# One wo load, the small MLP's end and the stage signals of a staged loop, in a gated attention and token-mixer decode kernel

## The chip, the cores and the metric

The kernel runs on one core of one Trainium2 chip. The metric is the time of one execution on the device in microseconds, the median of several runs. A core has five engines that matter here: PE (matrix products), DVE (vector work), ACT (activations and copies), POOL, and SP, which in this kernel issues nearly all of the transfers between the chip's main memory and the core. The transfers themselves are carried by 16 DMA engines.

## The reference

```python
x = A_x                                              # (1, 1, 448)
g = _sigmoid((x * gate_w).sum(-1, keepdims=True))
# A: 16 query heads, 8 KV heads, 65536 cached positions, head size 256
q = (x @ wq).reshape(B, Sq, Hq, Dh).transpose(0, 2, 1, 3)
k = jnp.repeat(k_cache, 2, axis=1); v = jnp.repeat(v_cache, 2, axis=1)
scores = jnp.einsum("bhqd,bhkd->bhqk", q, k) * (Dh ** -0.5)
o = jnp.einsum("bhqk,bhkd->bhqd", _softmax(scores), v)
a = o.transpose(0, 2, 1, 3).reshape(B, Sq, Hq * Dh) @ wo
# B: a token-mixing MLP on the same token
h = _layernorm(x)
u = _gelu(jnp.einsum("bsd,sf->bdf", h, w1) + b1)     # F = 1792
b = (jnp.einsum("bdf,fs->bds", u, w2) + b2).transpose(0, 2, 1)
return g * a + (1 - g) * b                           # (1, 1, 448), bfloat16
```

The two caches hold 268 MB each and are read once.

## The kernel before, in words

**Blocks.** The 8 KV heads times 65536 positions are cut into 32 blocks of 16384 positions, four to a head. A block has 8.39 MB of K, loaded by load_k in two halves into the two tiles kn0 and kn1 (L123), and 8.39 MB of V, loaded by load_v into the single tile vt (L129). All of them are issued by SP, in program order, on one queue. A tile is loaded again as soon as its last reader is done.

**A block's work.** score_block runs eight steps. A step transposes a slice of K on DVE (transposes, L384; steps 0 to 3 read kn0, steps 4 to 7 read kn1) and then forms eight products on PE (scores, L392). The transposed slices alternate between two buffers, so DVE's step i + 2 waits for PE's step i. softmax takes the maximum of the scores, rescales the running sums and writes the transposed weights pT (L449 to L488). products multiplies pT with V on PE (pv, L412) and adds up on DVE (accumulate, L493). A call may hand score_block a dictionary of hooks: functions whose instructions are put behind step i.

**The loop.** Blocks 0 to 29 run in a loop of 15 iterations with two blocks each (L560). An iteration has four stages: the scores of the first block and the load of its V; then the loads of the next block's K, its softmax and products; and the same two again for the second block. In every second such stage the loop also loads wo of one head (load_wo, L137) into the half wo_sb[:, 1], and in the last stage head_end works on finished heads and lets ACT copy wo_sb[:, 1] to wo_sb[:, 0] (L533), so that after iteration t the half 0 holds wo of head t.

**Stage signals.** The loop is of the staggered kind: an engine enters a stage only when all engines have signalled that they are finished with the stage two before it. By default an engine gives that signal when it comes to the next stage boundary, after it has waited for its own instructions (and on SP its own transfers) of that earlier stage. tc.previous_stage_wait(engine) puts the wait and the signal of one engine at another place in the stage. Waits at the boundary have line L560 in the profile.

**The tail.** Blocks 30 and 31 are written out. Block 30's scores have two hooks: mixer_tail behind step 1 (six DVE instructions, L334 to L345, that end the small MLP and form the gate) and gate_column behind step 2 (a product on PE, L543, that spreads the gate over the partitions, and its copy gcol on DVE, L546). SP issues 3 MB of block 30's V, the two halves of block 31's K, the other 5 MB of that V, and then block 31's V in eight pieces of 2 MB to 256 KB into the K tiles (load_v_last, L146), each when the transposes have freed its place. Behind them come two loads of wo, for heads 14 and 15. The end multiplies the last pieces (columns, L437), forms oT (L633), multiplies it with wo (L639: four products for head 14, four for head 15), copies the row (L645, L646) and stores it (L647).

An order written out by hand (seq) keeps each engine's instructions in program order.

Of the kernel before, what the change touches and what calls it, by code (L numbers as in the profile page):

```python
# [14 lines left out]
HQ = 16  # L15
HKV = 8
DH = 256
REP = HQ // HKV
# [5 lines left out]
NI = VP // NJ  # L24
# [7 lines left out]
def kernel(  # L32
# [28 lines left out]
    def seq(ins):  # L61
        e = ins.ins.engine
        if e in last:
            tc.add_manual_dep(
                ins.ins,
                last[e],
                mybir.DependencyInfo(
                    mybir.DependencyClass.NoSync, mybir.DependencyReason.DATA
                ),
                reason="program order",  # L70
            )
        last[e] = ins.ins.name
        return ins
# [62 lines left out]
    def load_wo(h, r):  # L136
        seq(nc.sync.dma_start(  # L137
            out=wo_sb[:, r],
            in_=A_wo.rearrange("(h p c) n -> h p c n", p=128, c=2)[bass.ds(h, 1)].rearrange(
                "o p c n -> (o p) c n"  # L140
            ),
        ))
# [162 lines left out]
    def place_q(pair):  # L305
        for a in range(NQ):
            quad = slice(32 * a, 32 * (a + 1))
            seq(nc.vector.tensor_copy(  # L308
                out=qz[quad, :, 2 * NI + 32 * a:2 * NI + 32 * a + REP],
                in_=qq_twice[quad, :, bass.ds(pair * REP, REP)],  # L310
            ))
# [21 lines left out]
    def mixer_tail():  # L333
        seq(nc.vector.tensor_scalar(  # L334
            out=gate[:], in0=ez[:], scalar1=1.0, scalar2=None, op0=ALU.add
        ))
        seq(nc.vector.reciprocal(out=gate[:], in_=gate[:]))
        seq(nc.vector.tensor_copy(out=b2f[:], in_=b2b[:]))
        seq(nc.vector.tensor_scalar(  # L339
            out=y_sb[:], in0=y_ps, scalar1=b2f[0:1, 0:1], scalar2=None, op0=ALU.add  # L340
        ))
        seq(nc.vector.tensor_scalar(
            out=rest[:], in0=y_sb[:], scalar1=gate[0:1, 0:1], scalar2=None, op0=ALU.mult
        ))
        seq(nc.vector.tensor_tensor(out=rest[:], in0=y_sb[:], in1=rest[:], op=ALU.subtract))  # L345
# [37 lines left out]
    def transposes(i):  # L383
        seq(nc.vector.transpose(  # L384
            out=kT_tiles[i % 2][:].rearrange("p j w k c -> p (j w k c)").bitcast(FP32),
            in_=k_tiles[i // 4][:, i % 4 * NJ:(i % 4 + 1) * NJ, :].rearrange("p j d -> p (j d)").bitcast(FP32),
        ))

    def scores(e, i):
        for w in range(NW):  # L390
            for c in range(2):
                seq(nc.tensor.matmul(  # L392
                    sc_tiles[e][:, :],
                    lhsT=qz[:, 2 * w + c, 2 * (NI - i):2 * (NI - i) + 128],
                    rhs=kT_tiles[i % 2][:, :, w, :, c],
                    start=(i == 0 and w == 0 and c == 0),
                    stop=(i == NI - 1 and w == NW - 1 and c == 1),
                ))

    def score_block(e, hooks={}):  # L400
        for i in range(NI):
            transposes(i)
            scores(e, i)
            if i in hooks:
                hooks[i]()
# [38 lines left out]
    def softmax(e, fill=None, may_begin=False, pair=None):  # L444
        fill = fill or [lambda: None] * 3
        sc_ps = sc_tiles[e]
        nb, nb_old = nb_tiles[e], nb_tiles[1 - e]
        al, pT = al_tiles[e], pT_tiles[e]
        seq(nc.vector.tensor_reduce(out=rmax[:], in_=sc_ps[:, :], op=ALU.max, axis=AXIS.X))  # L449
        if pair is not None:  # L450
            place_q(pair)
        fill[0]()
        seq(nc.tensor.transpose(sm_ps[0:1, 0:128], rmax[:, 0:1], ident_f[:, :]))  # L453
        fill[1]()
        seq(nc.vector.tensor_reduce(
            out=mnew[:],
            in_=sm_ps[0:1, 0:128].rearrange("o (a i r) -> o r a i", a=4, r=REP)[:, :, :, 0:NI],
            op=ALU.max, axis=AXIS.XY,
        ))
        if may_begin:  # L460
            seq(nc.vector.scalar_tensor_tensor(
                out=mrun[:], in0=mrun[:], scalar=caps[0:1, 1:2], in1=mnew[:],
                op0=ALU.min, op1=ALU.max,
            ))
        else:
            seq(nc.vector.tensor_tensor(out=mrun[:], in0=mrun[:], in1=mnew[:], op=ALU.max))  # L466
        seq(nc.tensor.matmul(  # L467
            sm_ps[:, 128:128 + REP], lhsT=ones_f[0:1, :], rhs=mrun[0:1, :], start=True, stop=True
        ))
        fill[2]()  # L470
        if may_begin:
            seq(nc.vector.tensor_tensor(
                out=nbo[:], in0=nb_old[:], in1=caps[:, 0:1], op=ALU.max
            ))
            nb_old = nbo
        seq(nc.vector.tensor_tensor_reduce(  # L476
            out=junk[:], in0=sm_ps[:, 128:128 + REP], in1=nval[:], scale=1.0, scalar=0.0,
            op0=ALU.mult, op1=ALU.add, accum_out=nb[:, 0:1],
        ))
        seq(nc.scalar.activation(  # L480
            out=p_sb[:, :], in_=sc_ps[:, :], func=ACT.Exp, scale=scale,
            bias=nb[:, 0:1], accum_out=den[:, 0:1],
        ))
        seq(nc.scalar.activation(
            out=al[:], in_=nb_old[:], func=ACT.Exp, scale=-1.0, bias=nb[:, 0:1]
        ))
        seq(nc.vector.transpose(out=pT[:, :], in_=p_sb[:, :]))  # L487
        seq(nc.vector.scalar_tensor_tensor(  # L488
            out=lsum[:], in0=lsum[:], scalar=al[:, 0:1], in1=den[:], op0=ALU.mult, op1=ALU.add
        ))  # L490
# [51 lines left out]
    def gate_column():  # L542
        seq(nc.tensor.matmul(  # L543
            sm_ps[:, 200:201], lhsT=ones_f[0:1, :], rhs=gate[0:1, 0:1], start=True, stop=True
        ))
        seq(nc.vector.tensor_copy(out=gcol[:], in_=sm_ps[:, 200:201]))  # L546
# [10 lines left out]
    mixer_sum()  # L557

    last.clear()
    with tc.For_i(0, HQ - 1, 1, iteration_sync="staggered") as t:  # L560
        for e in range(2):
            if e:
                tc.stage_boundary()
            score_block(e)
            load_v(2 * t + e)
            tc.stage_boundary()
            load_k(2 * t + e + 1, 0)
            load_k(2 * t + e + 1, 1)
            if e == 0:
                load_wo(t, 1)  # L570
                softmax(e, may_begin=True)
                products(e)
            else:
                softmax(e, pair=t + 1)
                denominators()
                products(e)
                head_end()
                turn()
    last.clear()

    for n in (L - 1, L):
        if n < L:
            score_block(n % 2, {1: mixer_tail, 2: gate_column})
        else:
            score_block(n % 2, {1: result_base, 2: lambda: pv(L - 1, 0), 3: lambda: pv_one(L - 1, 2)})
        if n == L - 1:
            load_v(n, 0, 48)
            load_k(L, 0)
            load_k(L, 1)
            load_v(n, 48, VP)  # L590
        else:
            load_v_last(L)
            for h in range(HQ - REP, HQ):
                load_wo(h, h - (HQ - REP))
        if n < L:
            softmax(n % 2)
        else:
            def rest_base():
                for k in range(2):
                    seq(nc.tensor.matmul(  # L600
                        f_rows[k], lhsT=ident_f[0:1, 0:1], rhs=base[0:1, k * MC:(k + 1) * MC],
                        start=True, stop=False, tile_position=(0, 32 * k),
                    ))
                pv(L - 1, 2, range(4, NJ))

            softmax(n % 2, [lambda: pv_one(L - 1, 3), lambda: pv(L - 1, 2, range(4)), rest_base])
            seq(nc.vector.tensor_scalar(
                out=lsv[:], in0=val[:], scalar1=lsum[:, 0:1], scalar2=None, op0=ALU.mult
            ))
            pv(L - 1, 3)  # L610
            accumulate((L - 1) % 2)
            seq(nc.tensor.matmul(
                sm_ps[:, 456:456 + REP], lhsT=ones_f[:, :], rhs=lsv[:, :], start=True, stop=True
            ))
            seq(nc.vector.reciprocal(out=rdv[:], in_=sm_ps[:, 456:456 + REP]))
            seq(nc.vector.tensor_scalar(
                out=rdv[:], in0=rdv[:], scalar1=gcol[:, 0:1], scalar2=None, op0=ALU.mult
            ))
# [59 lines left out]
```

## Time and profile before

| | |
|---|---|
| median of 3 runs | 1268.74 us (1267.89 to 1269.64) |
| the profiled execution | 1268.93 us |
| its span, first to last instruction | 1267.1 us |
| PE busy | 806.4 us (64%) |
| DVE busy | 707.7 us (56%) |
| ACT busy | 58.6 us (5%) |
| read from main memory | 544.45 MB, 430 GB/s over the span |
| mean granted TensorE clock | 0.807 |

The span runs from the first instruction to the last; the execution's own time has some 1.8 us around it. In the profile a line such as "vt<-in_A_v_cache_dram" names a tile and what is written into it. In the chain of waits, each piece is what the next one waited for; "issue" is time in which the engine waited for nothing that the profile shows. In a timeline a row has its start, its length, the engine and line, the tiles, and the number of instructions that are merged in it; the brackets give the idle time before it and what ended it. In a table of windows the columns are the stretch and its length, the busy time of PE, PE's weight loads, DVE, ACT and POOL (with counts), the granted clock, the DMA share and GB/s. The DMA share of a short window can be over 1, since a packet is counted whole where it starts.

### The profile page before, as it was taken

The numbers are of one execution on the slowest core, as the hardware profiler recorded it, in microseconds if no ns is written. First come the engines' busy times: TensorE is split into PE (matmuls) and PEld (weight loads), VectorE is DVE, ScalarE is ACT, GpSimd is POOL, SyncE is SP. The second block draws the span as 40 slices with busy tenths as digits, with TensorE's granted clock in tenths as the row PEclk, the third lists the DMA queues.
The fourth block names the chain that finished last, engine by engine and source line by source line (L and its number), as shares of the span: only waits on it lengthen the run. The fifth ranks groups of instructions, "written<-read, shape, count | busy, mean of one in ns | idle before, by whom it ended". The sixth has DMA issues, their size and how long they took to land.

```text
span 1267.1 us, 12204 instructions
## 1 busy us (share of the span) xinstructions
PE 806.4 (64%) x4689; PEld 321.2 (25%) x4689; DVE 707.7 (56%) x754; ACT 58.6 (5%) x131; POOL 1.7 (0%) x7
## 2 busy tenths in 40 slices
PE   3767665766656566566675675755657665676676
PEld 1222222222222222222222222222222222222223
DVE  4566545565445665456654556644566544665483
ACT  4000000000000000000000000000000000000000
POOL 0000000000000000000000000000000000000000
PEclk9888778788778787787877788777888778787687
DMA  9999999999999999999999999999999999999998
GB/s 413 414 437 444 429 439 418 435 432 446 434 418 437 431 450 432 432 420 432 449 432 435 418 433 434 445 435 418 438 430 447 435 430 424 430 446 435 418 419 343
DMA packets 18306, 544.59 MB, mean 430 GB/s; under 512 B 2421, under 2 KB 4600, under 8 KB 5112
## 3 DMA queue, kind: packets, MB, share of 16 engines
q1 hardware_dynamic: 17858, 544.45, 99.6%
q8 instruction: 6, 0.10, 0.0%
q10 hardware_dynamic: 438, 0.01, 0.0%
q14 instruction: 4, 0.03, 0.0%
HBM read 544.45 MB, written 0.00 MB: 430 GB/s over the span
## 4 chain that ended last, share of the span: by engine, by line
DMA 75%; issue 18%; PE 2%; DVE 2%; SPq 1%; ACT 0%; DVEq 0%
DMA vt<-in_A_v_cache_dram 73%; DMA kn<-in_A_v_cache_dram 2%; DVE kT L384 1%; PE sc L392 1%; PE pv_ps L412 1%; SPq L560 0%; SPq L129 0%; PE hd_ps L528 0%; PE f L639 0%; ACT p_sb L480 0%; DVE acc L493 0%; SPq L146 0%; DVE rmax L449 0%; DVE y_sb L339 0%; PE hd_ps L514 0%
## 5 line engine op out<-in xcount | busy, mean ns | idle before, releaser
L392 PE MATMUL sc<-kT,qz 128*128 128x512 bf16 x2048 | 550.9, 419 | 217.3 <-DVE kT L384 217.1
L384 DVE STREAM_TRANSPOSE kT<-kn 128x2048 f32<-128x2048 f32 x256 | 571.2, 2283 | 109.4 <-DMA kn<-in_A_k_cache_dram 52.6
L392 PEld LDWEIGHTS <-qz 128*128 128x128 bf16 x2048 | 212.7, 104 | 556.1 <-issue 379.4
L412 PE MATMUL pv_ps<-vt,pT 128*4 128x512 bf16 x1968 | 172.5, 526 | 129.0 <-DMA vt<-in_A_v_cache_dram 127.2
L493 DVE SCALAR_TENSOR_TENSOR acc<-acc,al,pv_ps 128x512 f32<-128x512 f32 x31 | 23.2, 748 | 266.5 <-PE pv_ps L412 266.5
L412 PEld LDWEIGHTS <-pT 128*4 128x4 bf16 x2000 | 58.7, 108 | 235.1 <-issue 190.0
L480 ACT ACTIVATE p_sb<-sc,nb 128x512 bf16<-128x512 f32 x32 | 22.0, 687 | 975.6 <-DVE nb L476 975.6
L449 DVE TENSOR_REDUCE rmax<-sc 128x1 f32<-128x512 f32 x32 | 22.1, 692 | 63.6 <-PE sc L392 63.6
L487 DVE STREAM_TRANSPOSE pT<-p_sb 128x512 bf16<-128x512 bf16 x32 | 22.8, 711 | 27.1 <-ACT p_sb L480 27.1
L499 PE MATMUL hd_ps<-lsum,same 128*128 128x1 f32 x30 | 7.4, 315 | 28.8 <-DVE lsum L488 28.8
L467 PE MATMUL sm_ps<-mrun,ones_f 1*128 1x2 f32 x64 | 12.1, 256 | 21.2 <-DVE mrun L466 12.9
L453 PE MATMUL sm_ps<-ident_f,rmax 128*1 128x128 f32 x32 | 8.6, 270 | 24.5 <-DVE rmax L449 24.5
L533 ACT COPY wo_sb<-wo_sb 128x896 bf16<-128x896 bf16 x15 | 14.1, 937 | 199.1 <-PE hd_ps L528 199.1
L514 PE MATMUL hd_ps<-esc,acc 128*128 128x2 f32 x60 | 9.5, 263 | 14.1 <-DVE acc L493 14.1
L528 PE MATMUL hd_ps<-wo_sb,oT 128*1 128x448 bf16 x60 | 17.9, 393 | 0.0
L532 DVE TENSOR_TENSOR a_acc<-a_acc,hd_ps 1x448 f32<-1x448 f32 x15 | 9.1, 608 | 14.5 <-PE hd_ps L528 14.5
L467 PEld LDWEIGHTS sm_ps<-mrun,ones_f 1*128 1x128 f32 x64 | 9.4, 182 | 27.4 <-DVE mrun L466 16.3
L499 PEld LDWEIGHTS hd_ps<-lsum,same 128*128 128x128 f32 x30 | 6.1, 253 | 30.1 <-DVE lsum L488 30.1
L514 PEld LDWEIGHTS hd_ps<-esc,acc 128*128 128x128 f32 x60 | 8.2, 196 | 21.6 <-DVE acc L493 21.6
L476 DVE CUSTOM_DVE_ANT_0 junk<-sm_ps,nval 128x2 f32<-128x2 f32 x32 | 5.1, 160 | 14.0 <-PE sm_ps L467 14.0
L453 PEld LDWEIGHTS sm_ps<-ident_f,rmax 128*1 128x1 f32 x32 | 2.5, 79 | 40.2 <-DVE rmax L449 40.2
L308 DVE COPY qz<-qq 32x16 bf16 (+1 forms) x64 | 10.5, 164 | 1.4
(114 smaller groups left out, 149.5 us busy)
## 6 DMA issues: line engine op xcount, KB each, us to landing
kn<-in_A_k_cache_dram SPq DMA_DIRECT2D x63, 4096.0 KB, 27.3
vt<-in_A_v_cache_dram SPq DMA_DIRECT2D x1, 5120.0 KB
kn<-in_A_k_cache_dram SPq DMA_DIRECT2D x2, 2048.0 KB, 11.9
kn<-in_A_v_cache_dram SPq DMA_DIRECT2D x2, 2048.0 KB, 20.9
wo_sb<-in_A_wo_dram SPq DMA_DIRECT2D x17, 224.0 KB, 27.3
vt<-in_A_wq_dram SPq DMA_DIRECT2D x1, 3072.0 KB, 10.3
vt<-in_A_v_cache_dram SPq DMA_DIRECT2D x1, 3072.0 KB
kn<-in_A_v_cache_dram SPq DMA_DIRECT2D x3, 1024.0 KB, 20.4
```

What stands on the lines that cost most here:

```text
L384: seq(nc.vector.transpose(out=kT_tiles[i % 2][:].rearrange("p j w k c -> p (j w k c)").bitcast(FP32), in_=k_tiles[i // 4][:, i % 4 * NJ:(i ...
L392: seq(nc.tensor.matmul(sc_tiles[e][:, :], lhsT=qz[:, 2 * w + c, 2 * (NI - i):2 * (NI - i) + 128], rhs=kT_tiles[i % 2][:, :, w, :, c], star ...
L412: seq(nc.tensor.matmul(dst[32 * grp:32 * grp + 2 * REP, :, :], lhsT=pT[:, 32 * jj + 2 * REP * ip:32 * jj + 2 * REP * (ip + 1)], rhs=pairs( ...
L449: seq(nc.vector.tensor_reduce(out=rmax[:], in_=sc_ps[:, :], op=ALU.max, axis=AXIS.X))
L467: seq(nc.tensor.matmul(sm_ps[:, 128:128 + REP], lhsT=ones_f[0:1, :], rhs=mrun[0:1, :], start=True, stop=True))
L480: seq(nc.scalar.activation(out=p_sb[:, :], in_=sc_ps[:, :], func=ACT.Exp, scale=scale, bias=nb[:, 0:1], accum_out=den[:, 0:1],))
L487: seq(nc.vector.transpose(out=pT[:, :], in_=p_sb[:, :]))
L493: seq(nc.vector.scalar_tensor_tensor(out=acc[:], in0=acc[:], scalar=al_tiles[e][:, 0:1], in1=src[:, :, :], op0=ALU.mult, op1=ALU.add,))
L499: seq(nc.tensor.matmul(hd_ps[:, 460:461], lhsT=same[:].rearrange("p a r -> p (a r)"), rhs=lsum[:, 0:1], start=True, stop=True,))
L514: seq(nc.tensor.matmul(o_ps[c], lhsT=acc[:, e, :].rearrange("p (d c) -> p c d", c=2)[:, c, :], rhs=weights[:, e, :], start=(start and e == ...
L528: seq(nc.tensor.matmul(a_ps, lhsT=oT[:, c, r:r + 1], rhs=wo_sb[:, r, c, :], start=(r == 0 and c == 0), stop=(r == REP - 1 and c == 1),))
L533: seq(nc.scalar.copy(out=wo_sb[:, 0], in_=wo_sb[:, 1]))
```

## The change

In the two score stages of each iteration, ACT's signal for the stage before is given at the head of the stage, and PE's and DVE's behind step 4 of the eight. In the tail, mixer_tail and gate_column are no longer hooks of block 30's scores but follow its softmax. wo of head 14, which iteration 14 leaves in wo_sb[:, 0], is not loaded a second time.

```diff
     last.clear()
+    def early_signals(i):
+        def both():
+            tc.previous_stage_wait(mybir.EngineType.PE)
+            tc.previous_stage_wait(mybir.EngineType.DVE)
+        return {i: both}
+
     with tc.For_i(0, HQ - 1, 1, iteration_sync="staggered") as t:
         for e in range(2):
             if e:
                 tc.stage_boundary()
-            score_block(e)
+            tc.previous_stage_wait(mybir.EngineType.Activation)
+            score_block(e, early_signals(NI // 2))
             load_v(2 * t + e)
             tc.stage_boundary()
             load_k(2 * t + e + 1, 0)
@@
     for n in (L - 1, L):
         if n < L:
-            score_block(n % 2, {1: mixer_tail, 2: gate_column})
+            score_block(n % 2)
         else:
             score_block(n % 2, {1: result_base, 2: lambda: pv(L - 1, 0), 3: lambda: pv_one(L - 1, 2)})
@@
             load_v_last(L)
-            for h in range(HQ - REP, HQ):
-                load_wo(h, h - (HQ - REP))
+            load_wo(HQ - 1, 1)
         if n < L:
             softmax(n % 2)
+            mixer_tail()
+            gate_column()
         else:
```

## The prediction

> **What bounds the kernel now.** I read the page first (slices and queues), then the chain that ended last, then SP's timeline, then short windows in the tail, and last the trace's DMA packet records (start, length and size of each packet). The page:
>
> ```profile
> DMA  9999999999999999999999999999999999999998
> ...
> DMA packets 18306, 544.59 MB, mean 430 GB/s; under 512 B 2421, under 2 KB 4600, under 8 KB 5112
> ...
> q1 hardware_dynamic: 17858, 544.45, 99.6%
> q8 instruction: 6, 0.10, 0.0%
> ```
>
> Packets fill 99.6% of 16 DMA engines' span. PE is busy 64% and DVE 56%, so neither bounds. The chain of waits shows it again: V transfers of 29 to 34 us and short issues between them.
>
> ```profile
> 603.77 33.72 DMA vt<-in_A_v_cache_dram
> 637.70 8.74 issue
> ...
> 681.99 33.44 DMA vt<-in_A_v_cache_dram
> ```
>
> V lands at 603.77 + 33.72 = 637.49 and, two blocks on, at 681.99 + 33.44 = 715.43. In those 77.94 us the queue moved four 8.389 MB tensors and one 0.229 MB wo load, 33.78 MB: 433.5 GB/s, and other pairs of blocks differ by 0.05 us. Is the queue ever empty? SP's timeline in the loop:
>
> ```profile
> 647.02 0.33 SPq L129 DMA_DIRECT2D vt<-in_A_v_cache_dram  x1
> 667.83 0.94 SPq L123 DMA_DIRECT2D kn<-in_A_k_cache_dram  x2
> 668.97 0.33 SPq L137 DMA_DIRECT2D wo_sb<-in_A_wo_dram  x1
> 681.99 0.33 SPq L129 DMA_DIRECT2D vt<-in_A_v_cache_dram  x1
> ```
>
> The V issued at 647.02 lands at 676.17 (647.02 + the chain's 29.15). K is issued 8.3 us before that, and the next V 13.5 us before that K ends (676.17 + 8.389 MB / 433.5 GB/s = 695.5). In the other half of the iteration K comes 9.9 us (627.63 against 637.49) and V 9.8 us ahead. The loop, 1170 of 1267 us, is one unbroken stream with 8 us to spare.
>
> The tail is not quite that. After block 29's V (landed 1183.07) there come 33.55 MB of K and V, 77.4 us at 433.5, so 1260.5; the last products on V start at 1262.80. Those 2.3 us are all that scheduling can win there. One part shows in half-microsecond windows (the last two columns are DMA share and GB/s):
>
> ```profile
> 1207.00:1207.50 0.50, 0.31 (x2) 0.19 (x2) 0.50 (x2) 0.00 (x0) 0.00 (x0) 1.00 0.46 197
> 1207.50:1208.00 0.50, 0.50 (x4) 0.20 (x3) 0.50 (x1) 0.00 (x0) 0.00 (x0) 1.00 0.24 98
> 1208.00:1208.50 0.50, 0.50 (x4) 0.20 (x3) 0.50 (x1) 0.00 (x0) 0.00 (x0) 1.00 2.34 672
> ```
>
> Most engines run dry for a microsecond, until the K load of block 31 arrives. SP had issued it at 1207.16, right after block 30's fourth transpose freed its tile:
>
> ```profile
> 1193.64 4.50 DVE L384 STREAM_TRANSPOSE kT<-kn 128x2048 f32<-128x2048 f32 x2 [0.16 <-PEq L560]
> ...
> 1199.62 0.61 DVE L345 TENSOR_TENSOR rest<-y_sb,rest 1x448 f32<-1x448 f32 x1
> 1200.17 2.29 DVE L384 STREAM_TRANSPOSE kT<-kn 128x2048 f32<-128x2048 f32 x1
> 1204.76 0.16 DVE L546 COPY gcol<-sm_ps 128x1 f32<-128x1 f32 x1 [2.30 <-PE sm_ps L543]
> 1204.83 4.50 DVE L384 STREAM_TRANSPOSE kT<-kn 128x2048 f32<-128x2048 f32 x2
> ```
>
> **The MLP's end.** It leaves a score block in which it delays DVE. In the loop the third and fourth transposes start 6.03 and 8.94 us after the first (653.33 and 656.24 against 647.30). Here they start 6.53 and 11.19 after it: mixer_tail's six DVE instructions (1198.07 to 1200.23) cost 0.50, and gcol, which waits 2.30 us for a PE product queued behind scores(2), makes it 2.25. Without both, K of block 31 is issued at 1207.16 - 2.25 = 1204.9. Its first packets came 1.0 us after issue (1208.13 in the packet records), so they can start at 1205.9; the first engine runs dry at 1207.24: cover 1.3 us.
>
> What is that worth at the end? By the packet records the engines finished the 3 MB load before it between 1207.24 and 1209.66 (median 1207.65). The next 2 x 2 MB, 9.69 us without a gap, were done at 1218.42 on the first engine and 1218.60 on the median: lost 1.49 and 1.26 us. The two latest engines (1209.29 and 1209.66) lost nothing. Only the engine that ends last counts. It fetched 16 KB of program code at 1245.23 (0.93 us, one of q8's six packets), which put it 1.4 us back, 1.0 behind the next (1247.25 against 1246.23); before that it ran with the pack that had lost 1.2. With the gap closed it is 1.2 us earlier, and an engine that lost nothing, 1.25 us ahead of it, is next. So the term lies between +0.2 (the fetch falls on one of the late engines) and -1.25. I take -0.9, near the row of the engine that did end last, with some allowance for another fetch pattern.
>
> Where the block goes, DVE gets it back: softmax starts 2.25 earlier, then 2.16 us of mixer_tail and some 0.6 for the gate product (0.38), gcol (0.16) and their signals; block 31's first transpose moves from 1221.55 to about 1222.1. Queued behind are block 31's scores on PE and SP's eight V pieces, issued from 1226.08 to 1242.86. The first piece is not needed before block 30's V ends at 1240.4, the last not before 1259: cover 14 us, cost nothing. If that cover were gone it would cost 0.5.
>
> **wo of head 14.** The load goes away, 128 packets of 74 ns, 8 on each engine: 0.59 us of queue time, but behind the last V piece, so V gains nothing. SP saves one 0.33 us issue while it idles. What does gain:
>
> ```profile
> 1263.42 1.04 PE L639 MATMUL f<-wo_sb,oT 128*1 128x224 bf16 x8 [0.25 <-DVE oT L633]
> ...
> 1263.93 0.09 PEld L639 LDWEIGHTS <-oT 128*1 128x1 bf16 x3 [0.24 <-issue]
> ```
>
> The products start in pairs 0.14 us apart (1263.42, 1263.56), so the fifth could start at 1263.70. It starts at 1263.93, just after the second load landed on the slowest engine (1263.89 by its semaphore). One load ends 0.57 earlier and that stall is gone: -0.23. What is late next is oT itself.
>
> **Mid-stage signals.** ACT's signal moves to the head of the score stage, PE's and DVE's behind the fifth of eight steps. SP enters the next stage earlier, so the first K load of a block (its tile is free after four transposes) goes out some 4 to 5 us earlier; the second still waits for the eighth transpose. wo and the next V stay behind them in the same order. The stream was never dry there: 0. Bounds: at the first K of the loop (issued 47.60, wanted from 49.82) the window 49.8 to 50.6 shows a share of 0.87, a possible -0.1 to -0.26 on early engines. Upward, PE and DVE now wait at step five for their own previous stage, over some 14 us before; behind DVE's wait stand three transposes and PE's last scores. Even the 0.5 us that one hook cost would sit under 8.3 us of cover. Should that be gone, it would cost 30 x 0.5 = 15.
>
> By the Trainium skill, "DMA: Bandwidth & Descriptors", Specifications, the fabric into SBUF ends at 435 GB/s; the loop's 433.5 agrees. By it alone (an estimate) no earlier issue in the loop could win more than 0.3% of 1170 us, some 4 us; my sum has none.
>
> **Sum.** -0.9 - 0.23 + 0 = -1.1. The profiled execution took 1268.93 (span 1267.1 and 1.8 around it), 0.2 above the median of 1268.74. So 1267.8 for its like, 1267.6 from the median; I say 1267.7.
>
> **Rivals.**
> *The gap closes for the wrong engines* (0.33): a code fetch meets an engine that was already late, or new addresses move a fetch to the end. For it: three of 16 engines are late, and one fetch (1259.23) lies 3 us before the end. Then only wo's 0.2 remains, or less: 1268.5, between 1268.0 and 1269.4.
> *A queued load has a fixed cost of its own* (0.05): if the removed one cost the 1.0 us from issue to first packet besides its 0.59, and the forecast's 0.9 came on top, 1268.74 - 2.5 = 1266.2. Against it: the last two 256 KB pieces let their products start at 1262.18 and 1262.80, 0.62 apart, and bytes alone make 0.61. The Trainium skill, same page, "Anatomy of one DMA — SWDGE (gpsimd) path", fits 2.0 us plus the bytes to a load issued by GpSimd; by it, as an estimate, this load would be 2.5 us. The row speaks against that for SP's queued loads.
> *The loop's code no longer stays on the chip* (0.04), slower: no 16 KB fetch lies between 50.7 and 1198.6, and the tail, about one iteration's code, made four of 16 KB and three of 8 KB. If moved or added signal instructions push the loop past what is kept, each iteration fetches as much: 4 x 1.4 + 3 x 0.35 = 6.7 us on one or another engine, 15 iterations 100 us, over 16 engines 6.3: about 1275. It decides once any fetch repeats in the loop. Against it: signals move, they do not multiply.
> *The early signals give nothing because SP waits for its own transfers*: also possible, and the time is the forecast's.
>
> **How the numbers follow.** Forecast 0.55 (1266.8 to 1268.3), the first rival 0.33, fixed cost 0.05, code 0.04, unnamed 0.03. The range 1266.2 to 1269.4 holds the first two with their bounds. 0.2% is 2.5 us, about what a measurement of this kernel can tell from no change. Below 1266.2: the fixed cost and 0.01 unnamed, 0.06; above 1271.3: code and 0.01, 0.05; within: 0.89.
>
> **What would show it.** Right: no slice with a DMA share under 0.7 near 1207; block 31's first K issue near 1204.9; no PE pause between the fourth and fifth product of L639; the loop's pair of K issues parted by 4 us, yet V landings still 77.9 us apart per iteration. Wrong: V landings closer together, q8 rows above some ten packets, or the last product on V still starting at 1262.8 with the gap gone.

## The result and the profile after

The changed kernel takes 1266.32 us, the median of 21 runs between 1266.14 and 1266.50. The kernel before, beside it, takes 1268.59 (21 runs, 1267.14 to 1270.06). The ratio is 0.9982, 95% interval 0.9976 to 0.9988: 2.3 us or 0.18% faster. Two things changed, then: the median, and the scatter, which fell from 2.9 us to 0.4. The profiled execution took 1266.22 (span 1264.4). Its page:

```profile
DMA  9999999999999999999999999999999999999998
...
DMA packets 18162, 544.36 MB, mean 431 GB/s; under 512 B 2405, under 2 KB 4456, under 8 KB 4968
...
q1 hardware_dynamic: 17714, 544.22, 99.7%
q8 instruction: 6, 0.10, 0.0%
```

The queue has 0.23 MB less in it and is as full as before; the code fetches (q8) are again six. The loop, from the chain of waits and from SP's timeline:

```profile
604.84 32.12 DMA vt<-in_A_v_cache_dram
...
681.37 33.52 DMA vt<-in_A_v_cache_dram
```

```profile
646.40 0.33 SPq L129 DMA_DIRECT2D vt<-in_A_v_cache_dram  x1
660.62 6.54 SPq L123 DMA_DIRECT2D kn<-in_A_k_cache_dram  x2
667.36 0.33 SPq L137 DMA_DIRECT2D wo_sb<-in_A_wo_dram  x1
681.37 0.33 SPq L129 DMA_DIRECT2D vt<-in_A_v_cache_dram  x1
```

V lands at 636.96 and 714.89, 77.93 us apart (77.94 before). The pair of K issues is now stretched over 6.5 us: its first half goes out early, and the stream of transfers in the loop does not notice. In the tail, DVE in block 30's scores, and the windows that showed the queue running dry:

```profile
1199.01 2.31 DVE L384 STREAM_TRANSPOSE kT<-kn 128x2048 f32<-128x2048 f32 x1 [1.47 <-PE sc L392]
1201.82 6.70 DVE L384 STREAM_TRANSPOSE kT<-kn 128x2048 f32<-128x2048 f32 x3 [0.49 <-PE sc L392]
```

```profile
1207.00:1207.50 0.50, 0.50 (x4) 0.23 (x3) 0.50 (x1) 0.00 (x0) 0.00 (x0) 1.00 1.30 541
1207.50:1208.00 0.50, 0.50 (x4) 0.25 (x3) 0.50 (x1) 0.00 (x0) 0.00 (x0) 1.00 0.53 229
```

A share of 0.53 beside one of 1.30 looks like a gap, and by the letter of the prediction (no share under 0.7) it is one. But a 32 KB packet lasts 1.2 us and is counted whole where it starts, so half-microsecond windows swing by themselves. Ten microseconds tell it better. First the kernel before, then the changed one:

```profile
1206.00:1216.00 10.00, 7.66 (x33) 3.11 (x33) 9.90 (x5) 0.00 (x0) 0.00 (x0) 1.00 0.93 383
```

```profile
1206.00:1216.00 10.00, 7.97 (x34) 3.06 (x32) 7.65 (x6) 0.00 (x0) 0.00 (x0) 1.00 1.04 447
```

383 GB/s over ten microseconds is 1.2 us of transfer short of the loop's 433.5; the changed kernel is not short of it. The last products on V start at 1260.24 instead of 1262.80, and the store is issued at 1262.26 instead of 1264.94.

By the packet records the gain on the engine that ends last builds up like this: its V of block 29 ends at 1182.13 instead of 1182.65, 0.5 us of which 0.3 are there after the loop's first K load (61.50 against 61.80); its last V piece ends at 1259.84 instead of 1262.45, so 2.1 us more in the tail. Some 0.2 us of the first part appear around 110 to 130 us, in one V transfer of the kernel before; no run explains them.

### The profile page after: what moved, and what is told of

Read it like the earlier page. It is cut to its first block, busy times and chain, and to the rows that moved or that the text cites. A ratio compares the mean times of both kernels' runs of the same rounds, so it can differ in the third digit from the quotient of the medians.

```text
span 1264.4 us, 12203 instructions
## 1 busy us (share of the span) xinstructions
PE 809.1 (64%) x4689; PEld 322.6 (26%) x4689; DVE 707.9 (56%) x754; ACT 58.6 (5%) x131; POOL 1.7 (0%) x7
## 4 chain that ended last, share of the span: by engine, by line
DMA 75%; issue 19%; PE 3%; DVE 1%; SPq 1%; ACT 0%; DVEq 0%
DMA vt<-in_A_v_cache_dram 73%; PE sc L392 2%; DMA kn<-in_A_v_cache_dram 1%; DVE kT L384 1%; PE pv_ps L412 1%; SPq L566 0%; SPq L129 0%; PE hd_ps L528 0%; PE f L647 0%; ACT p_sb L480 0%; DVE acc L493 0%; SPq L146 0%; DVE rmax L449 0%; DVE y_sb L339 0%; PE hd_ps L514 0%
## 5 line engine op out<-in xcount | busy, mean ns | idle before, releaser
L412 PE MATMUL pv_ps<-vt,pT 128*4 128x512 bf16 x1968 | 175.5, 534 | 126.6 <-DMA vt<-in_A_v_cache_dram 124.8
```

The source lines that it names most:

```text
L412: seq(nc.tensor.matmul(dst[32 * grp:32 * grp + 2 * REP, :, :], lhsT=pT[:, 32 * jj + 2 * REP * ip:32 * jj + 2 * REP * (ip + 1)], rhs=pairs( ...
```

## The experiments

Twelve kernels ran, each beside the kernel before on the same chip; "spread" is lowest to highest run. The theory after the first four runs was L: a K load that is issued too shortly before the DMA engines want it slows their packets, by an amount that changes from run to run. It happens at two places, the loop's first K and block 31's K, and either alone scatters the end.

**The three parts, and all but one.** Their theory G put most of the gain down to the gap near 1207 us. Each of them is the kernel before with some hunks of the change's diff: e1 the move of the MLP's end, e2 the wo load left out, e3 the early signals, e4 the last two. Their core lines:

```diff
# e1
-            score_block(n % 2, {1: mixer_tail, 2: gate_column})
+            score_block(n % 2)
+            mixer_tail(); gate_column()          # behind softmax(n % 2)
# e2, e4
-            for h in range(HQ - REP, HQ):
-                load_wo(h, h - (HQ - REP))
+            load_wo(HQ - 1, 1)
# e3, e4
-            score_block(e)
+            tc.previous_stage_wait(mybir.EngineType.Activation)
+            score_block(e, early_signals(NI // 2))
```

> Only the MLP's end is moved behind block 30's softmax; both wo loads and the loop's default signals stay. Theory G (the gap in the DMA queue near 1207 us is what cost time): most of the change's 2.3 us comes from here, 1.4 to 2.0 us below the kernel before (ratio 0.9984 to 0.9989), K of block 31 issued near 1204.9, no window under 0.7 of DMA share near 1207, and the runs lie close together. Rival S (the earlier signals steady the stream): under 0.5 us. Rival F (any shift of the tail's code moves the code fetches and so the end): about as much as in the run that changes wo alone.

> Only the second load of wo of head 14 is left out. Theory G: 0.1 to 0.3 us, the pause before the fifth product of the last step goes, ratio 0.9997 to 1.0000, and the runs scatter as the kernel before does (some 3 us). Rival F: as much as the run that moves the MLP's end, 1 us or more in either direction, since the code behind shifts here too.

> Only the loop's signals are given in mid-stage. Theory G: 0.2 to 0.6 us, won once, at the first K load of the loop (last engine of that load done near 61.5 instead of 61.8), the blocks after it as far apart as before (77.9 us for two); the gap near 1207 and the scatter of the runs stay. Rival S: 1.5 us or more, with V landings closer together all through the loop.

> The change without the move of the MLP's end (signals and wo alone). Theory G: the sum of the two, 0.3 to 0.9 us below the kernel before, so over 1.2 us above the changed kernel; the runs scatter. Rival S: close to the changed kernel's 1266.3. Rival F: anywhere within 1.5 us of the kernel before.

Measured, with the kernel before at 1268.17 (1266.69 to 1269.66): e1 1267.23 (1266.73 to 1268.70), ratio 0.9994 (0.9985 to 1.0003); e2 1268.39, ratio 1.0002 (0.9993 to 1.0011); e3 1267.87 (1267.36 to 1269.96), ratio 0.9998 (0.9989 to 1.0007); e4 1268.67 (1267.04 to 1269.20), ratio 1.0001 (0.9992 to 1.0010). No part alone, and not the pair in e4, is clear of the kernel before; yet together they give 2.3 us and a spread of 0.4. The parts do not add up, so theory G in its first form fell for e1 (0.9 instead of 1.4 to 2.0, and the runs did scatter) and for e4 (0.5 above the kernel before instead of 0.3 to 0.9 below it). Rival S fell with e3.

The profiles say why. In e1 the windows at 1206 are good (434 GB/s), but the first K load of the loop is not. SP's timeline of e1:

```profile
47.91 0.95 SPq L123 DMA_DIRECT2D kn<-in_A_k_cache_dram  x2
49.06 0.33 SPq L137 DMA_DIRECT2D wo_sb<-in_A_wo_dram  x1
```

The first DMA engine is done with the V before it at 49.83, 1.9 us later. The ten microseconds behind, for e1:

```profile
50.00:60.00 10.00, 5.67 (x67) 2.14 (x68) 2.29 (x9) 0.96 (x3) 0.00 (x0) 0.83 0.98 398
```

and for the changed kernel, where SP issues the first half at 40.78:

```profile
50.00:60.00 10.00, 4.00 (x66) 1.84 (x67) 2.10 (x8) 0.96 (x3) 0.00 (x0) 1.00 1.03 441
```

The DMA share hardly differs (0.98, 1.03): the engines are not idle, their packets are longer. The packet records have 1.3 to 2.7 us for many 32 KB packets that take 1.213 elsewhere. The mirror image is e3, with 441 GB/s at 50 and this at 1206:

```profile
1206.00:1216.00 10.00, 9.18 (x33) 3.50 (x33) 8.89 (x4) 0.00 (x0) 0.00 (x0) 0.83 0.99 412
```

The table counts from the packet records the 32 KB packets over 1.33 us ("slow") at both places, with the lead: from SP's issue to the first engine's being done with the load before. One or two slow packets in each are the ones behind a 16 KB code fetch. For block 31's K the lead is that of its first half, while the count takes in both halves. The second half has a lead of 3.7 us or more in e1, in the changed kernel and in e5 to e8 and e10, of 2.5 in the kernel before, e2, e4 and e9, and of 1.4 in e3 and e12, where it holds more than half of the slow packets. Between the two places the profiles of e1 to e10, e12 and both kernels have no slow 32 KB packet but one behind a code fetch between 1195 and 1200 us, and no K load there has a lead under 4.3 us.

The runs come from several chips: the median of the kernel before is 1268.17 beside e1 to e4, 1268.54 beside e5 to e8, 1268.34 beside e9 to e11 and 1268.10 beside e12. A lead and a count are those of one profiled execution. That of e3 and of e12 is the longest of their runs, that of e1 is 0.02 us below its longest, and that of e6 is the shortest.

| kernel | first K: lead us, slow | block 31's K: lead us, slow | median (spread) us |
|---|---|---|---|
| before | 2.2, 6 | 0.1, 18 | 1268.59 (1267.14 to 1270.06) |
| e1 MLP's end only | 1.9, 18 | 3.1, 2 | 1267.23 (1266.73 to 1268.70) |
| e2 wo only | 2.0, 17 | -0.8, 20 | 1268.39 (1267.55 to 1269.47) |
| e3 signals only | 9.6, 1 | 0.9, 31 | 1267.87 (1267.36 to 1269.96) |
| e4 signals and wo | 9.2, 1 | 1.0, 18 | 1268.67 (1267.04 to 1269.20) |
| after | 9.1, 1 | 2.8, 2 | 1266.32 (1266.14 to 1266.50) |
| e5 both wo loads | 9.5, 1 | 3.6, 2 | 1266.27 (1266.11 to 1266.52) |
| e6 signals late | 2.8, 3 | 3.7, 2 | 1266.54 (1266.00 to 1268.32) |
| e7 first half only | 8.8, 1 | 3.7, 2 | 1266.27 (1266.00 to 1266.60) |
| e8 mixer_tail as hook | 8.6, 1 | 3.6, 2 | 1266.24 (1266.03 to 1266.50) |
| e9 delay of three | 9.3, 1 | 1.5, 6 | 1266.44 (1266.22 to 1267.07) |
| e10 code shifted | 8.6, 0 | 3.8, 1 | 1266.40 (1266.23 to 1266.64) |
| e12 delay of four | 9.0, 1 | 1.3, 28 | 1267.26 (1266.12 to 1268.24) |

**Is it the first K's lead, and only that, that the signals give?** Both start from the changed kernel:

```diff
# e6
-            score_block(e, early_signals(NI // 2))
+            score_block(e, early_signals(NI - 1))
# e7
-            tc.previous_stage_wait(mybir.EngineType.Activation)
-            score_block(e, early_signals(NI // 2))
+            if e == 0:
+                tc.previous_stage_wait(mybir.EngineType.Activation)
+            score_block(e, early_signals(NI // 2) if e == 0 else {})
```

> The change with PE's and DVE's signals behind the last step of eight instead of the fifth. Theory L: the first K of the loop is issued near 47.5 again, some 2 us ahead, its packets after 49.8 are slowed, and the runs scatter like those with the MLP's end moved alone: median 1266.8 to 1267.5, a spread of over 1 us. Rival M (it is not the lead of that one load but some other effect of the mid-stage signals in the loop, such as fewer waits on SP): the same would be seen only if that effect needs the fifth step too; if the signal's being given inside the stage is enough, 1266.3.

> The change with the mid-stage signals in the first score stage of an iteration only; the second keeps the default. The first K of the loop is issued from the first half. Theory L: as the changed kernel, 1266.2 to 1266.5 with a spread under 0.5 us, since the signals matter for that one load. Rival S (they matter all through the loop): half of the effect is gone, 0.4 us or more slower.

Beside them the kernel before has 1268.54. e7 has 1266.27 with a spread of 0.6, ratio 0.9984 (0.9975 to 0.9993): half of the signals do all of it. e6 has 1266.54, ratio 0.9990 (0.9981 to 0.9999), and scatters up to 1268.32, which the changed kernel never does, though it gives its signals inside the stage too. Its profile happens to be of its shortest run (1266.00), with a lead of 2.8 us and three slow packets, where the changed kernel has one. So 2 to 3 us seem to lie at the edge, though no profile of one of e6's longer runs is there to show the slow packets. That the signals count through this one load alone is argued, not shown: e6 and e7 change the signals of all iterations. For it speaks that the loop's other K loads have no slow packets with the signals or without. The median came out just below what theory L had expected.

**wo and the hook.** e5 is the changed kernel with both wo loads, e8 with mixer_tail back as a hook behind step 1 (gate_column stays behind the softmax).

```diff
# e5
-            load_wo(HQ - 1, 1)
+            for h in range(HQ - REP, HQ):
+                load_wo(h, h - (HQ - REP))
# e8
-            score_block(n % 2)
+            score_block(n % 2, {1: mixer_tail})
-            mixer_tail()
```

> The change with wo of head 14 loaded a second time again. Theory L (a K load that is issued less than some 2.3 us before the first DMA engine wants it slows packets, at the first K of the loop and at block 31's K; either place alone scatters the end, and only both together make it steady): both K loads keep their lead, so the runs stay within some 0.5 us of each other, and the load costs what it costs at the end, 0.1 to 0.25 us: 1266.4 to 1266.6. Rival F (code shifts): scatter as in the kernel before, about 1267 to 1268.

> The change with the six instructions of mixer_tail put back behind step 1 of block 30's scores; gate_column stays behind the softmax. Block 31's K is issued 0.5 us later, 2.3 us ahead of the first engine's need. Theory L: at the edge: a few slowed packets, 1266.3 to 1266.9, with more spread than the changed kernel. Prediction's cover (1.3 us beyond the 1.0 us to the first packet): no effect at all, 1266.3.

e5 has 1266.27, ratio 0.9982 (0.9973 to 0.9991), and e8 1266.24, ratio 0.9984 (0.9975 to 0.9993), both with a spread under 0.5: neither the load nor the six instructions cost anything that runs can show. e8 did not test the edge it was meant for, because K of block 31 kept a lead of 3.6 us. DVE in e8's block 30:

```profile
1198.23 0.61 DVE L345 TENSOR_TENSOR rest<-y_sb,rest 1x448 f32<-1x448 f32 x1
1198.77 11.06 DVE L384 STREAM_TRANSPOSE kT<-kn 128x2048 f32<-128x2048 f32 x5
```

The hook's instructions lie mostly where DVE would wait 1.47 us for PE anyway. All of the old delay came from gate_column, whose copy waited for a PE product behind step 2's scores.

**Taking the lead away in another manner.** e9 puts three statistics instructions on DVE behind step 2 of block 30's scores in the changed kernel, e12 four (results not used):

```diff
+    def hold():
+        for _ in range(3):                     # e12: range(4)
+            seq(nc.vector.bn_stats(out=stats[:], in_=xf[:]))
...
-            score_block(n % 2)
+            score_block(n % 2, {2: hold})
```

> The changed kernel with three statistics instructions on DVE (0.63 us each, their result is not used) behind step 2 of block 30's scores. DVE waits some 0.5 us for PE there, so block 31's K is issued about 1.4 us later and its lead falls from 2.8 to 3.6 us to about 1.4 to 2.2. Nothing else of the change is undone. Theory L: slowed packets near 1207 (some ten instead of two), and the runs scatter upward: 1266.3 to 1268.5, median 0.3 us or more above the changed kernel. Rival P (the gate product of the old hook cost PE or DVE time that the end waited for, not the lead): no effect, 1266.3.

> The changed kernel with four such statistics instructions on DVE behind step 2 of block 30's scores (results not used), one more than in the run before: block 31's K is issued some 0.9 us ahead of the first engine's need, as in the run without the move of the MLP's end (1.0 us there). Theory L in its plain form (the lead alone sets the scatter): median 1267.5 to 1268.7 and a spread of 1.5 us or more, as that run. Theory L with a price that grows with the missing lead: 1266.6 to 1267.2. Rival P (the old hook's gate product did something besides delaying the load): 1266.4 to 1266.6 with a spread under 1 us, as with three instructions.

e9: 1266.44, spread 0.85, ratio 0.9986 (0.9977 to 0.9995); e12: 1267.26, spread 2.1, ratio 0.9990 (0.9981 to 0.9999). e9 came out milder than theory L had expected: six slow packets instead of some ten, and 0.1 us at the median instead of 0.3 or more. Nothing of the change is undone in e12 but the lead of block 31's K, and its runs reach from the changed kernel's best to 2 us above it. Rival P is out. The medians suggest a price that grows with the missing lead rather than switching on: 2.8 us of lead in the changed kernel, 1.5 in e9 with 0.1 us more at the median, 1.3 in e12 with 0.9, 1.0 in e4 with 2.3. With one profile for each, and medians from different chips, the order is a hint; what is clear is e12's spread, 2.1 us against 0.4.

The lead itself varies. In e12's profile the two halves of block 31's K go out 10.0 us apart, in the changed kernel 8.8. SP's timeline of e12, then of the changed kernel:

```profile
1205.51 10.31 SPq L123 DMA_DIRECT2D kn<-in_A_k_cache_dram  x2
```

```profile
1204.16 9.10 SPq L123 DMA_DIRECT2D kn<-in_A_k_cache_dram  x2
```

In e12 the granted clock stood at 0.50 around 1207 us, where the changed kernel has 1.00:

```profile
1207.00:1207.50 0.50, 0.50 (x2) 0.15 (x1) 0.50 (x1) 0.00 (x0) 0.00 (x0) 0.50 1.70 655
```

PE was late with its scores, DVE waited 1.09 us for them, and the second half followed later. e3's profile shows the same (0.78 us). So some of the scatter can come from where the clock falls; the kernel before has both a late load and a clock of 1.00 there, so the clock is not needed for it.

**Code fetches.** e10 adds 64 small products on PE in the preamble of the changed kernel (results not used).

```diff
+    for _ in range(64):
+        seq(nc.tensor.matmul(hd_ps[:, 100:101], lhsT=ones_b[:, :], rhs=ones_b[:, 0:1], start=True, stop=True))
```

> The changed kernel with 64 small products on PE in its preamble (result not used, PE idles there), which move all of PE's code behind them by 128 instructions, half of a 16 KB fetch. Theory L: the fetches in the tail move by several us, the runs stay steady (spread under 0.6 us), the median within 0.5 us of the changed kernel, either way. Rival F (where the fetches fall decides the end): a median 0.6 us or more away, or runs that scatter.

1266.40 with a spread of 0.4, ratio 0.9985 (0.9976 to 0.9994). The 16 KB fetch of the changed kernel at 1207.14 came at 1232.74 instead, those at 1244.57 and 1256.83 at 1247.59 and 1258.94, and the end moved by 0.1 us. So to move the fetches does nothing to the changed kernel, and rival F is out as a rival to the lead.

The fetches are nevertheless part of the price. The packet records of each profile give the time at which the last engine is done with block 30's V, and with the last piece of block 31's V:

| kernel | block 30's V | last piece | between, us |
|---|---|---|---|
| before | 1241.37 | 1262.45 | 21.08 |
| e1 MLP's end only | 1241.09 | 1262.13 | 21.04 |
| e2 wo only | 1242.26 | 1262.94 | 20.68 |
| e3 signals only | 1242.40 | 1263.46 | 21.06 |
| e4 signals and wo | 1240.48 | 1261.53 | 21.05 |
| e9 delay of three | 1240.22 | 1260.29 | 20.07 |
| e12 delay of four | 1241.72 | 1261.90 | 20.18 |
| after | 1240.22 | 1259.84 | 19.62 |
| e5 to e8, e10 | 1240.03 to 1240.42 | 1259.66 to 1260.05 | 19.62 to 19.63 |

Followed packet by packet, most engines take 19.62 us for this stretch, and the two on which a 16 KB fetch falls take 21.03 in the changed kernel. There these two were done with block 30's V at 1238.49 and 1238.51, 1.7 us ahead of the last engine, and are still 0.3 ahead of it at the end: the fetch is hidden. In the seven kernels with a lead of 2.2 us or less at one of the places or both, the end comes 0.4 to 1.5 us later than 19.62 us behind block 30's V. A late load takes from most engines the time that they were ahead of the last one: the first half of block 31's K ends between 1216.64 and 1218.45 on the 16 engines in the changed kernel, between 1218.43 and 1219.60 in the kernel before. Then a fetch shows. This is read from one profile of each kernel; no run leaves a fetch out.

**A larger K transfer.** e11 loads K of every second block in one piece:

```diff
+    kn = kvpool.tile([128, VP, DH], BF16, name="kn")
+    k_tiles = [kn[:, i * KP:(i + 1) * KP, :] for i in range(2)]
...
-            load_k(2 * t + e + 1, 0)
-            load_k(2 * t + e + 1, 1)
+            if e == 0:
+                load_k(2 * t + e + 1, 0)
+                load_k(2 * t + e + 1, 1)
+            else:
+                seq(nc.sync.dma_start(out=kn[:], in_=rows("k", 2 * t + e + 1)))
```

> The changed kernel, but K of every second block (issued in the loop's second half) is loaded in one transfer with 64 KB a partition instead of two with 32 KB. The packet records have 2418 ns for 64 KB and 1213 ns for 32 KB, 8 ns less for the same bytes, and a V load ends 19.32 us after the one before it on an engine, two K halves 19.37: 15 such loads save 0.7 to 1.0 us if the stream of packets alone sets the time: 1265.3 to 1265.7, steady. Its load is issued some 6 us later than its first half was, still 9 us ahead. If a lead under 10 us mattered in the loop: scatter, and no gain.

1273.59, ratio 1.0041 (1.0028 to 1.0055): 5.3 us slower than the kernel before. In the loop it did gain, 0.35 us by block 29's V (1181.78 on the last engine against 1182.13). But block 30's K now lands whole or not at all:

```profile
1201.60 4.50 DVE L385 STREAM_TRANSPOSE kT<-kn 128x2048 f32<-128x2048 f32 x2 [10.68 <-DMA kn<-in_A_k_cache_dram]
```

Its transposes start 8.6 us later than in the changed kernel, so block 31's K is issued at 1212.33, and the queue, with 3 MB of V to live on, is truly empty:

```profile
1208.00:1210.00 2.00, 2.00 (x8) 0.73 (x7) 1.90 (x2) 0.00 (x0) 0.00 (x0) 0.80 0.00 0
1210.00:1212.00 2.00, 1.84 (x8) 0.71 (x8) 2.00 (x1) 0.00 (x0) 0.00 (x0) 1.00 0.00 0
```

It is the same load that is late, now by 6 us; the 0.7 to 1.0 us that had been expected of the larger transfers came out as 0.35 in the loop and drowned in that. No version clearly below the changed kernel came out; e5, e7 and e8 equal it within 0.1 us.

## Why the prediction was right or wrong

**What bounds, and the sign.** Right: the loop's blocks stayed 77.9 us apart, all of the gain lies outside the loop's steady part, and K of block 31 was issued at 1204.16 (1204.9 was foreseen). The gain of 2.3 us was foreseen as 1.1, and that is a matter of two terms. The measured 1266.32 lies below the forecast's own 1266.8 to 1268.3 and 0.1 above the low end of the whole range, next to the 1266.2 of the rival with a fixed cost, which the runs did not bear out. That it lies in the range at all is in part luck. The pair of K issues came out 6.2 us apart (4 foreseen). The "8 us to spare" in the loop were counted to the landing on the last engine; to the first engine's end, as the first K was counted, the shortest lead of a K load in the loop behind it is 5.3, which was enough all the same.

**"The stream was never dry there: 0."** This step failed, at one load. The prediction saw that the loop's first K was issued at 47.60 and wanted from 49.82, and bounded its cost by the share of one window and by the idle 0.26 us of the earliest engine. But engines need not be idle to lose time: with 2 us of lead their packets lasted 1.3 to 2.7 us instead of 1.2. In the profile of before this cost only 0.3 us on the last engine, with fewer slow packets (6) than in e1 and e2 (18, 17) at nearly the same lead; a single profiled execution did not show that the term varies.

**-0.9 for the gap at 1207.** Right place, wrong size. In the profiles the tail's part is 2.1 us. The way in which the gap costs was read rightly: the latest engines lost nothing in it, most others did, and a fetch then made one of these the last. Of the 2.6 us between the two profiles' last pieces, 1.15 were there at the end of block 30's V, and 1.46 come behind it, where that fetch falls; the changed kernel hides its fetches there. What failed is the bound of -1.25. It took an engine that was next, 1.25 us ahead, as fixed. But in the kernel before, a fetch at 1198.55 had put that engine back (11.10 us for half a K load instead of 9.68); in the changed kernel the fetch at 1197.17 fell on the engine that was first. The scatter of the runs fits places that are dealt anew in each execution with a late load, and with them what a fetch costs; with one profile of each kernel that is argued, not shown.

The parts show it at the median. Without the signals, moving the MLP's end gives 0.9 (e1); with them it gives 2.3 (e4 against the changed kernel). In e1's profile the last engine is 0.87 us later than in the changed kernel behind the loop's first K, still so at block 29's V (1183.00 against 1182.13), and another 1.4 behind block 30's V.

**1.0 us from issue to first packet,** used as all the lead that a load needs, was too small: the 2.2 us at the loop's first K were not enough, about 3 are. For block 31's K the prediction worked with 1204.9 against 1207.24, a lead of 2.3. It came out as 2.8, since block 30's transposes also began 0.6 earlier (1193.03 against 1193.64); whether 2.3 would have been steady no run shows.

**0.50 for mixer_tail's instructions.** Wrong: e8 has them back at no cost. They delay the third transpose, but the fourth waits for PE in any case.

**-0.23 for wo.** The pause is gone, as the changed kernel's last step shows (eight products start without the break before the sixth weight load):

```profile
1260.87 0.46 PEld L647 LDWEIGHTS <-oT 128*1 128x1 bf16 x8 [0.34 <-DVE oT L641]
1260.87 0.91 PE L647 MATMUL f<-wo_sb,oT 128*1 128x224 bf16 x8 [0.26 <-DVE oT L641]
```

0.91 us of busy time against 1.04 in the kernel before and 1.03 in e5: 0.12, and in the medians of e5 and the changed kernel nothing.

**The rivals.** That the gap closes for the wrong engines did not come true, and with long leads the place of the fetches decides nothing (e10). With a short lead what that rival describes is at work, as the table of block 30's V shows. A fixed cost of a queued load fell with e5: 0.05 us the other way. The Trainium skill, "DMA: Bandwidth & Descriptors", section "Anatomy of one DMA — SWDGE (gpsimd) path", has 2.0 us of it for loads that GpSimd issues; for this load, issued by SP behind others, the runs show none. Code that no longer stays on the chip did not happen (q8 stays at six packets).

## What to carry to other kernels

When transfers bound a kernel, ask of every load not only whether the queue still has work when it is issued, but for how long: here a lead of about 3 us or more was free, and 2 us or less cost up to 2.3 us at the median, even where hardly an engine stood still. Two such places hide each other, since either alone is enough to spoil the end: repair them together before judging the parts. Ask also how far the other engines are ahead of the last one, since that is what hides a fetch. And look at the scatter of the runs as well as at the median; here it was the first sign that something random had been in the way, and once it was gone the runs lay within 0.4 us.

## What the runs showed of the hardware that was not expected

A load issued 1 to 2 us ahead of need makes DMA packets longer (1.3 to 2.9 us instead of 1.213 for 32 KB) rather than leaving gaps between them; why, no run here tells. A 16 KB code fetch of 0.93 us sets the engine on which it falls back by 1.4 us (21.03 us instead of 19.62 over the last pieces). The 16 engines keep such differences for over a thousand microseconds: in e1 the engines' ends of the loop's first K lay up to 2.3 us apart, and those of block 29's V still did (60.10 to 62.37, 1180.73 to 1183.00).
